# Moving one early load behind a weight piece, and releasing the weight queue on half of a query load

## The chip, the cores and the metric

The kernel runs on one core of a Trainium2 chip. The metric is the device time of one execution in microseconds. The span in a profile, from the first to the last instruction, is some 1.8 us shorter than the time of the same execution.

## The reference, cut to what matters

Gated linear attention over 768 positions, then a mixture of four experts, all of them applied to every row.

```python
f = 1 / (1 + exp(-f_logit))
for t in range(S):                        # B=4, H=8, S=768, D=48
    state = f[:, :, t, :, None] * state + k_t (outer) v_t
    y[:, :, t] = q_t @ state
x = y as [B*S, H*D]                       # 3072 x 384
for e in range(4):
    h = maximum(x @ w1[e], 0)             # 384 -> 1024: "first projection"
    out += p[:, e:e+1] * (h @ w2[e])      # 1024 -> 384: "second projection"
```

The kernel cuts the 768 positions into six chunks of 128 and puts the attention of one chunk beside the expert matmuls of another. Only chunk 0's attention has nothing to hide behind.

## The kernel before: the parts concerned

The engines have these names in the profiles: PE (TensorE, the matmuls), ACT (ScalarE), DVE (VectorE), POOL (GpSimd), SP (SyncE). A small planner orders the instructions of every engine from rough costs. The chunk 0 inputs are loaded by SyncE (SP), one load of 192 KB for each tensor and batch, 192 bytes (one head of one position) in a row. The weights are loaded by GpSimd (POOL), which casts them to bf16 on the way: pieces 0 to 3 are halves of the first two experts' w1, pieces 4 and 5 halves of the first expert's w2 (384 KB each as written), pieces 6 to 10 whole matrices of 768 KB.

```python
def load(c, nm, b, n):                        # c: chunk, nm: f k q v, b: batch
    ins[c, nm, b] = nc.sync.dma_start(out=tl(nm, c, b // 2)[:, hh(b, n), :],
                                      in_=srcs[nm][c, :, b * H:(b + n) * H, :])
    if (c, nm, b) == (1, "f", 1):
        after(ins[c, nm, b], ins["w", w_gate])        # w_gate: piece 8

def load_w(i, e, which, ks, cols):
    ...
    ins["w", i] = nc.gpsimd.dma_start(out=w[:, e, ks, cols], in_=r[e][:, ks, cols])
    if i == 0:
        after(ins["w", 0], ins[0, "q", B - 1])        # weights start here
    if i == w_last:
        after(ins["w", i], ins[1, "k", 0])

def mm_h(c, e, fc, n0, n1):                   # first projection, needs w1
    for kk in range(KD):
        nc.tensor.matmul(out=..., lhsT=w1_sb[:, e, kk, ...], rhs=tl("xT", c)[:, kk, n0:n1], ...)

def mm_o(c, e, nt, fcs, part, cols):          # second projection, needs w2
    for fc in fcs:
        nc.tensor.matmul(out=..., lhsT=tl("h", c, e, ...)[:, fc, ...], rhs=w2_sb[:, e, fc, cols], ...)

for i, x in enumerate("f0 k0 q0 f1 k1 q1 f2 f3 k2 q2 v0 k3 q3 v1 v2 v3".split()):
    add_load(0, x[0], int(x[1]), 1, -1000 + i)
add_load(1, "f", 0, 1, -980, cost=0.1)        # the second chunk's first gate logits
```

`after(x, y)` makes transfer x wait until y has landed.

## Time and profile before

| | before |
|---|---|
| median of 3 runs before the prediction (lowest, highest) | 299.21 us (299.13, 299.32) |
| the execution whose profile was read: time, span | 300.17 us, 298.4 us |
| TensorE (PE) busy in it | 287.4 us |
| PE waiting for weight pieces 0, 1, 4 in it | 0.24, 0.73, 1.15 us |

The prediction quotes the lines of this profile.

### The profile page before, as it was taken

The page shows a single profiled execution, that of the slowest core. Times are in us where ns is not written, and L with a number is a line of the kernel's source. Part 1 is how long each engine was busy: PE and PEld are TensorE (multiplying, and loading weights), DVE is VectorE, ACT ScalarE, POOL GpSimd, SP SyncE. Part 2 cuts the span into 40 slices and gives each one's busy share as a digit, 9 for nine tenths or more (in the row PEclk, how much of TensorE's full clock was granted, in tenths as well). Part 3 has the DMA queues.
Part 4 walks back from the last instruction along what each step waited for, and adds up shares of the span by engine and source line. Part 5 has one row for each costly group of instructions (what it writes and reads, how often), then busy time and mean ns, then how long its engine had stood idle before and what let it go on. Part 6 is the DMA issues. An engine that isn't in the chain of part 4 may idle for free.

```text
span 298.4 us, 5544 instructions
## 1 busy us (share of the span) xinstructions
PE 287.4 (96%) x2132; PEld 170.6 (57%) x2160; DVE 126.8 (43%) x247; ACT 176.1 (59%) x325; POOL 105.5 (35%) x179
## 2 busy tenths in 40 slices
PE   6898899999999999999999999999999999999995
PEld 2466455567777776455555555555555555555553
DVE  6766003585675584036375444332532322201223
ACT  5786573857765676877465574555465544465440
POOL 5397301329498159325548453234220000000000
PEclk9999999999999999999999999999999999999999
DMA  7999999996979979996989962102431100200003
GB/s 146 218 174 195 207 208 188 199 197 168 173 158 193 209 140 181 195 221 118 195 160 205 191 113 35 29 0 64 108 69 38 26 2 26 79 2 0 0 0 108
DMA packets 136462, 36.82 MB, mean 123 GB/s; under 512 B 126812, under 2 KB 135644, under 8 KB 136436
## 3 DMA queue, kind: packets, MB, share of 16 engines
q1 hardware_dynamic: 129348, 30.14, 50.9%
q0 software_dynamic: 7088, 6.33, 13.6%
q8 instruction: 17, 0.28, 0.4%
q14 instruction: 9, 0.07, 0.1%
HBM read 31.51 MB, written 4.72 MB: 121 GB/s over the span
## 4 chain that ended last, share of the span: by engine, by line
PE 88%; DMA 5%; SPq 3%; POOL 1%; issue 1%; DVE 0%
PE ps_m L379 42%; PE ps_m L364 39%; DMA w_sb<-in_moe_w_dram 4%; SPq L232 3%; PE ps_t L320 2%; PE ps_t L335 1%; PE ps_t L331 1%; DMA q<-in_q_dram 1%; PE ps_t L268 1%; POOL w_sb L239 1%; PE ps_t L341 1%; PE ps_t L305 0%; SPq L247 0%; DVE o L386 0%; PE ps_t L360 0%
## 5 line engine op out<-in xcount | busy, mean ns | idle before, releaser
L375 ACT ACTIVATE h<-ps_m 128x512 bf16<-128x512 f32 (+1 forms) x192 | 102.4, 538 | 93.7 <-PE ps_m L364 89.9
L379 PE MATMUL ps_m<-w_sb,h 128*128 128x384 bf16 (+1 forms) x776 | 151.7, 324 | 1.4 <-DMA w_sb<-in_moe_w_dram 1.1
L364 PE MATMUL ps_m<-xT,w_sb 128*128 128x512 bf16 (+1 forms) x670 | 150.1, 341 | 2.1 <-DMA w_sb<-in_moe_w_dram 1.0
L379 PEld LDWEIGHTS <-h 128*128 128x128 bf16 x776 | 75.0, 98 | 60.0 <-DMA w_sb<-in_moe_w_dram 1.6
L386 DVE SCALAR_TENSOR_TENSOR o<-ps_m,pn,o 128x384 f32<-128x384 f32 (+1 forms) x73 | 44.7, 612 | 111.9 <-PE ps_m L379 105.6
L364 PEld LDWEIGHTS <-w_sb 128*128 128x128 bf16 x696 | 65.5, 98 | 43.7 <-DMA w_sb<-in_moe_w_dram 1.4
L296 POOL TENSOR_TENSOR qk<-q,e 128x384 bf16<-128x384 f32 x19 | 22.5, 1189 | 36.3 <-ACT e L288 32.5
L324 DVE TENSOR_TENSOR AT<-ps_t,mask 128x512 bf16<-128x512 f32 x48 | 29.9, 682 | 5.8 <-PE ps_t L320 5.8
L355 POOL TENSOR_TENSOR Sf<-Sf,egs 48x192 f32<-48x192 f32 x40 | 20.1, 503 | 32.6 <-DVE Sf L348 30.6
L288 ACT ACTIVATE e<-ps_t 128x384 f32<-128x384 f32 x48 | 26.6, 665 | 4.1 <-PE ps_t L268 2.9
L373 DVE TENSOR_SCALAR h<-ps_m 128x256 bf16<-128x256 f32 (+1 forms) x40 | 20.0, 510 | 18.3 <-PE ps_m L364 16.1
L296 POOL TENSOR_TENSOR qk<-k,e 128x384 bf16<-128x384 f32 x20 | 20.2, 1015 | 9.3 <-ACT egs L290 4.6
L348 DVE TENSOR_TENSOR Sf<-Sf,ps_t 48x192 f32<-48x192 f32 x40 | 14.0, 351 | 11.4 <-PE ps_t L341 10.7
L239 POOL DMA_DIRECT2D w_sb<-in_moe_w_dram x11 | 9.0, 824 | 21.8 <-DMA k<-in_k_dram 18.5
L356 POOL CAST sb<-Sf 48x192 bf16<-48x192 f32 x40 | 13.6, 340 | 2.6
L388 ACT ACTIVATE o<-ps_m,pn 128x384 f32<-128x384 f32 x22 | 12.8, 581 | 2.8 <-PE ps_m L379 1.7
L293 POOL DMA_DIRECT2D egs<-e x16 | 9.0, 565 | 9.9 <-ACT e L288 9.9
L614 PE MATMUL ps_m<-busy 128*128 128x512 bf16 x32 | 10.5, 427 | 1.6 <-DVE busy L144 1.5
L226 ACT CAST yb<-ps_t 128x384 bf16<-128x384 f32 (+1 forms) x16 | 7.6, 472 | 7.5 <-PE ps_t L335 7.3
L260 ACT ACTIVATE ex<-f 128x768 f32<-128x768 f32 (+1 forms) x14 | 10.5, 748 | 2.3 <-DMA f<-in_f_logit_dram 2.2
L335 PE MATMUL ps_t<-vb,AT 128*128 128x48 bf16 x192 | 11.5, 184 | 0.2 <-DVE vb L228 0.2
L228 POOL CAST vb<-v 128x384 bf16<-128x384 f32 x18 | 9.7, 558 | 3.8 <-DMA v<-in_v_dram 3.7
(54 smaller groups left out, 123.9 us busy)
## 6 DMA issues: line engine op xcount, KB each, us to landing
out_dram<-o SPq DMA_DIRECT2D x23, 192.0 KB, 1.9
w_sb<-in_moe_w_dram POOLq DMA_DIRECT2D x5, 768.0 KB, 19.5
k<-in_k_dram SPq DMA_DIRECT2D x10, 384.0 KB, 4.7
q<-in_q_dram SPq DMA_DIRECT2D x10, 384.0 KB, 5.4
v<-in_v_dram SPq DMA_DIRECT2D x10, 384.0 KB, 5.4
f<-in_f_logit_dram SPq DMA_DIRECT2D x9, 384.0 KB, 5.0
w_sb<-in_moe_w_dram POOLq DMA_DIRECT2D x6, 384.0 KB, 9.4
f<-in_f_logit_dram SPq DMA_DIRECT2D x6, 192.0 KB, 3.8
```

The lines of the kernel that those rows point to most:

```text
L288: nc.scalar.activation(out=o, in_=i, func=AF.Exp, scale=1.0 if j else -1.0)
L296: engines[eng].tensor_tensor(out=tl("qk", c, b)[:, j, :, 0:D].rearrange("t (i r) d -> t i r d", r=2), in0=tl("qk"[j], c, b // 2)[:, hh(b), ...
L324: nc.vector.tensor_tensor(out=tl("AT", c, b)[:, r].rearrange("s i t -> s (i t)"), in0=tl("A", c, b, r).rearrange("s i t -> s (i t)"), in1= ...
L335: nc.tensor.matmul(out=y[:, h * D:(h + 1) * D], lhsT=AT[:, r, i, :], rhs=vb[:, h, :], start=(c == 0), stop=True, skip_group_check=True)
L348: nc.vector.tensor_tensor(out=Sf[rows, b], in0=Sf[rows, b], in1=KV[rows, :, r, :], op=ALU.add)
L355: nc.gpsimd.tensor_tensor(out=Sf[rows, b], in0=Sf[rows, b], in1=eg, op=ALU.mult)
L356: nc.gpsimd.tensor_copy(out=nb[rows, b, :, r * D:(r + 1) * D], in_=Sf[rows, b])
L364: nc.tensor.matmul(out=tl("hp", c, e, fc, n0)[:, n0:n1], lhsT=w1_sb[:, e, kk, fc * 128:(fc + 1) * 128], rhs=tl("xT", c)[:, kk, n0:n1], sta ...
L373: nc.vector.tensor_relu(out=dst, in_=src)
L375: nc.scalar.activation(out=dst, in_=src, func=AF.Relu)
L379: nc.tensor.matmul(out=tl("op", c, e, nt, part)[:, cols], lhsT=tl("h", c, e, half_of(c, nt * T))[:, fc, nt * T:(nt + 1) * T], rhs=w2_sb[:, ...
L386: nc.vector.scalar_tensor_tensor(out=o, in0=op, scalar=pe, in1=o, op0=ALU.mult, op1=ALU.add)
```

## The change

Its intent is to bring the first weights to PE sooner, in two ways. The last query load of chunk 0 is cut into two halves of four heads, and the weight queue waits for the first of them alone. The second chunk's first gate logits, 192 KB not needed before 50 us, no longer run beside the first weights: they wait until piece 6 has landed.

```diff
     def load(c, nm, b, n):
-        ins[c, nm, b] = nc.sync.dma_start(out=tl(nm, c, b // 2)[:, hh(b, n), :],
-                                          in_=srcs[nm][c, :, b * H:(b + n) * H, :])
+
+        for h in ((H // 2, H // 2) if (c, nm, b) == (0, "q", B - 1) else (n * H,)):
+            h0 = 0 if (c, nm, b) not in ins else h
+            op = nc.sync.dma_start(out=tl(nm, c, b // 2)[:, hh(b).start + h0:hh(b).start + h0 + h, :],
+                                   in_=srcs[nm][c, :, b * H + h0:b * H + h0 + h, :])
+            ins.setdefault((c, nm, b), op)
+        if (c, nm, b) == (1, "f", 0):
+            after(ins[c, nm, b], ins["w", 6])
@@
-    add_load(1, "f", 0, 1, -980, cost=0.1)
@@
     for i, (e, which, ks, cols) in enumerate(pieces):
+        if i == 7:
+            add_load(1, "f", 0, 1, -454.5, deps=wd[2, 1], cost=0.1)
```

## The prediction

> **What bounds the kernel now.** I read the page first: engine shares, slices, the chain that ended last. TensorE (PE) is busy for 287.4 of 298.4 us at a granted clock of 9 tenths or more in every slice, and the chain is PE for 88%.
>
> ```profile
> PE 287.4 (96%) x2132; PEld 170.6 (57%) x2160; DVE 126.8 (43%) x247; ACT 176.1 (59%) x325; POOL 105.5 (35%) x179
> PE   6898899999999999999999999999999999999995
> PE 88%; DMA 5%; SPq 3%; POOL 1%; issue 1%; DVE 0%
> ```
>
> The reader is to see that only the first slices of the PE row fall short of 9. So nothing but a wait of PE in the first 35 us can be won. I therefore took the chain in order of time, its first 75 us:
>
> ```profile
> 11.59 3.59 DMA q<-in_q_dram
> 15.18 0.30 issue
> 15.47 3.24 POOL w_sb L239 x4
> 18.72 12.54 DMA w_sb<-in_moe_w_dram
> 31.26 0.05 issue
> 31.30 1.47 PE ps_m L379 x8
> ```
>
> This is the path that sets the end: the last query load of chunk 0 (issued at 11.59, landed at 15.18) releases the weight queue on POOL; the fifth piece (number 4, the first half of the first expert's w2) is issued as the fifth there and lands at 31.26; PE then starts the second matmuls (L379) and is never again short of work. The timeline of PE shows how long it stood still before:
>
> ```profile
> 21.05 1.16 PE L364 MATMUL ps_m<-xT,w_sb 128*128 128x256 bf16 x9 [0.24 <-DMA w_sb<-in_moe_w_dram]
> ...
> 23.43 0.50 PE L364 MATMUL ps_m<-xT,w_sb 128*128 128x256 bf16 x3 [0.73 <-DMA w_sb<-in_moe_w_dram]
> ...
> 31.30 1.47 PE L379 MATMUL ps_m<-w_sb,h 128*128 128x384 bf16 x8 [1.15 <-DMA w_sb<-in_moe_w_dram]
> ```
>
> The bracket is PE's idle time: 0.24 + 0.73 + 1.15 = 2.12 us, all for pieces 0, 1 and 4. That sum is the ceiling of what earlier weights can bring. The waits of PE after 31.3 us come to one entry, this same 1.1 us; from 60 us on the view of waits lists none.
>
> The view of DMA issues, in windows around one issue each, gives landings as start plus time to landing: piece 0 at 15.47 + 5.5 = 21.0, piece 1 at 23.3, piece 2 at 25.6, piece 3 at 28.1, piece 4 at 31.3, piece 5 at 32.9, piece 6 at 36.7, piece 7 at 40.6, piece 8 at 44.2, piece 9 at 48.1, piece 10 at 59.4. The window about the first weight issue also holds the load that the change moves:
>
> ```profile
> w_sb<-in_moe_w_dram POOLq DMA_DIRECT2D x1, 384.0 KB, 5.5
> f<-in_f_logit_dram SPq DMA_DIRECT2D x1, 192.0 KB, 13.3
> ```
>
> The second chunk's first gate logits are issued at 15.08 and land at 28.4: all their 192 KB run beside pieces 0 to 3, before piece 4 lands.
>
> **What the Trainium skill says.** "DMA: Bandwidth & Descriptors", section "Issuing engines are not separate DMA queues": transfers from different engines end on the same 16 DMA engines and interleave. The trace agrees: between 20.5 and 31 us the DMA share is 1.18 to 1.39 and the rate 185 to 228 GB/s, while two queues run. Same page, section "Anatomy of one DMA": most of a fixed cost of about 2 us is the receipt at the end. The trace has stores landing in a median 1.9 us, and loads in 3.2 to 3.8 us under load; so a half load can't land much sooner by being half, only by standing earlier in the queue. "Perfetto Trace Analysis", section "DMA Optimizations": splitting may let some work start sooner if the DMA engines are generally idle. Here they are not (225, 233 and 187 GB/s in the half microseconds from 14 us), so I expect little of the split itself.
>
> **The change part by part.**
> (a) The split. The key load before it lands at 11.15 + 3.2 = 14.35 and the query load at 15.18, so 192 KB take 0.83 us of the queue. The half that ends first should land about 0.83 / 2 = 0.4 us sooner, at 14.8. POOL has been free since 12.24 + 1.00 = 13.24, so weight issues start near 15.05 in place of 15.47. Cost: one more SP issue (such issues take 0.4 to 1.3 us), with the value loads behind it; their landings (4.2 to 5.3 us after issue) are queued data, not issue time. The second half feeds a product on DVE that starts at 15.71, half a microsecond after the landing; no cost. In the built program the weights do wait on the first half, and each later load on the semaphore of one load later than before, all of them landed by then.
> (b) The gate logits leave. 192 KB (196.6 thousand bytes) at the 190 GB/s of 21 to 27 us is 196.6 / 190 = 1.03 us of DMA time that pieces 0 to 4 no longer share. Most of its benefit is there at piece 4; by piece 1 perhaps 0.4 us, as about half of it has then been sent.
> (c) They come back behind piece 6 (about 35.5 us), before the second gate load, which still waits for piece 8. Nothing else stands on the SP queue from 15 to 44.6 us, so blocking it costs nothing. Pieces 7 to 10 get the 1.0 us back and end about 0.4 us earlier than before.
> (d) The order of instructions. PE's is the same up to the middle of the second chunk, where two small matmuls (L268) go ahead of three transposes; ACT and DVE swap some evictions from there on. The amount of PE work is unchanged. I give this 0.
>
> Sum: piece 4 lands 0.4 + 1.0 = 1.4 us sooner, at 29.9. Would PE be ready? Its work ahead ended at 25.76 + 4.40 = 30.16, of which 0.73 us was the wait for piece 1. Piece 1 comes 0.4 + 0.4 = 0.8 us sooner, the piece 0 wait gives at most 0.24, so PE is ready at some 29.3 to 29.5, still before 29.9. So PE gains the full 1.4 us.
>
> Does it keep it? PE needs piece 5 at 33.9 (the half projections behind the first two, landed 32.9), piece 6 at 39.75 (36.7), piece 7 at 42.99 (40.6), piece 8 at 50.1 (44.2), piece 9 at 52.1 (48.1), piece 10 at 62.45 (59.4). Taking 1.4 us from the first column, and 1.4 (pieces 5, 6) or 0.4 us from the landings, leaves at least 1.0 us everywhere: the tightest are piece 5 with 1.0 and piece 7 with 41.6 against 40.2, 1.4 us. The second gate load landed at 49.4 and ACT reads it at 52.77; minus 1.4 it is still 2 us behind. So 299.21 - 1.4 = 297.8 us, 0.5% less.
>
> **The rivals.**
> First, the logits were hidden anyway: if they took slots that the weight queue could not use, removing them frees nothing. For it: the rate falls to 69 and 58 GB/s from 17.0 to 18.0 us with both queues loaded, so the engines are not always full. Against it: from 20.5 us on the share is over 1.2 without a gap, and pieces 1 to 3 are 2.3 to 2.5 us apart where 393 KB at 190 GB/s would take 2.07. It would leave (a) alone, 298.8 us.
> Second, PE takes over: chunk 0's own attention sets when the first projections can run. The transposed copies of batches 1 and 2 are done at 20.9 and of batch 3 at 22.8, and the value product at 20.44 stands ahead in PE's order. If pre-projection work can't move by more than the 0.3 us there, PE is ready at about 29.9: the gain is 1.2 to 1.3 us rather than 1.4, 298.0 us. If instead piece 4 is sooner than I think, this limit and the 2.12 us ceiling stop the gain: 297.1 us.
> Third, something in the middle gives it back: piece 7 late behind the returned logits, or a PE wait from the new order of evictions. For it: PE waits for nothing from 60 us on, so any change of order can only hurt there. Against it: margins of 1 us and more, and only 12 of the 4315 rows in PE's order differ. It would make 298.3 to 299.2 us.
>
> **Range and chances.** 1.4 us with (a) between 0.1 and 0.6 and (b) between 0.6 and 1.3 gives 0.7 to 1.9; adding a loss of up to 0.4 us at the lower end gives 297.0 to 298.9 us for 8 in 10. A gain over 2% (6.0 us) is three times the idle time there is: 0.01. A loss over 2% would need a new stall of 6 us, with loads issued in nearly the same order: 0.01. Within 2%: 0.98.
>
> **What would show it.** In the profile after: the first weight issue on POOL near 15.0 us; piece 4's landing, that is PE's first L379 matmul, at 29.9 in place of 31.3, with a wait of 0.3 to 0.7 us ahead of it; the moved load issued near 35.5 us; no PE wait over 0.2 us from there to the end; the end 1.4 us sooner. Step (a) is wrong if POOL starts within 0.1 us of 15.47; (b) is wrong if the distance from POOL's start to L379 (31.30 - 15.47 = 15.8 us) doesn't shrink to about 14.8; the keeping is wrong if L379 starts sooner by more than the end does.

## The result, and the profile after

| | before | after |
|---|---|---|
| median of 6 runs each, same chip | 299.17 us (298.57 to 300.38) | 298.67 us (298.32 to 298.92) |
| span of the profiled execution | 298.4 us | 296.9 us |

The ratio is 0.998, with a 95% interval of 0.996 to 0.9999. A ratio here is the mean time of one kernel's runs over that of the other's of the same rounds, so not quite the ratio of the medians. Executions over 1.5% slower than the fastest of the same kernel are left out of the means. The gain is real but small: 0.5 us of the forecast 1.4.

The two profiles say something else. Their spans differ by 1.5 us, as forecast. That is three times what the medians differ by.

The page of the changed kernel: the busy time of each engine, and the shares of the engines in the chain (the work that ended last, followed back from the last instruction to what released each step):

```profile
PE 287.3 (97%) x2132; PEld 170.7 (58%) x2160; DVE 127.6 (43%) x249; ACT 175.7 (59%) x323; POOL 105.6 (36%) x179
PE 91%; DMA 4%; SPq 3%; issue 1%; POOL 0%; DVE 0%
```

PE's work is the same; less of the chain is DMA (4% in place of 5%). The changed kernel's chain in order of time (start, us, what) where the weights enter it:

```profile
14.63 0.30 issue
14.93 0.92 POOL w_sb L245
15.85 7.52 DMA w_sb<-in_moe_w_dram
23.36 0.05 issue
23.41 0.50 PE ps_m L370 x3
```

The chain before went through four weight issues to piece 4 and to the second projections at 31.30. This one goes through a single issue and then the second: the transfer that is issued at 15.85 and lands at 23.36 is piece 1, the second half of the first expert's w1. From there on this stretch of the chain is PE alone. The timeline of PE in the changed kernel (start, us, engine and line, matmuls, idle time before them and what ended it; L370 is the first projection, L385 the second, which were L364 and L379 before; the edits of the experiments shift these numbers by a few lines):

```profile
21.54 1.16 PE L370 MATMUL ps_m<-xT,w_sb 128*128 128x256 bf16 x9 [1.15 <-DMA w_sb<-in_moe_w_dram]
23.41 0.50 PE L370 MATMUL ps_m<-xT,w_sb 128*128 128x256 bf16 x3 [0.22 <-DMA w_sb<-in_moe_w_dram]
29.97 1.46 PE L385 MATMUL ps_m<-w_sb,h 128*128 128x384 bf16 x8
```

There is no bracket on the third line: piece 4 landed at 29.2, and PE no longer waits for it. Piece 0 landed at 21.5 and piece 1 at 23.4, where they had landed at 21.0 and 23.4 before, although POOL had begun 0.54 us sooner.

### The profile page after: what moved, and what is told of

It reads as the page before. It is cut to its first block, busy times and chain, and to the rows that moved or that the text cites. A ratio compares the mean times of both kernels' runs of the same rounds, so it can differ in the third digit from the quotient of the medians.

```text
span 296.9 us, 5547 instructions
## 1 busy us (share of the span) xinstructions
PE 287.3 (97%) x2132; PEld 170.7 (58%) x2160; DVE 127.6 (43%) x249; ACT 175.7 (59%) x323; POOL 105.6 (36%) x179
## 3 DMA queue, kind: packets, MB, share of 16 engines
q0 software_dynamic: 7088, 6.33, 13.8%
## 4 chain that ended last, share of the span: by engine, by line
PE 91%; DMA 4%; SPq 3%; issue 1%; POOL 0%; DVE 0%
PE ps_m L385 42%; PE ps_m L370 41%; SPq L235 3%; DMA w_sb<-in_moe_w_dram 3%; PE ps_t L326 2%; PE ps_t L341 1%; PE ps_t L337 1%; PE ps_t L347 1%; PE ps_t L274 1%; DMA q<-in_q_dram 1%; POOL w_sb L245 0%; PE ps_t L311 0%; SPq L253 0%; DVE o L392 0%; PE ps_t L366 0%
## 5 line engine op out<-in xcount | busy, mean ns | idle before, releaser
L370 PE MATMUL ps_m<-xT,w_sb 128*128 128x512 bf16 (+1 forms) x670 | 150.1, 341 | 2.5 <-DMA w_sb<-in_moe_w_dram 1.4
L385 PE MATMUL ps_m<-w_sb,h 128*128 128x384 bf16 (+1 forms) x776 | 151.5, 324 | 0.2
L385 PEld LDWEIGHTS <-h 128*128 128x128 bf16 x776 | 75.1, 98 | 58.6
L370 PEld LDWEIGHTS <-w_sb 128*128 128x128 bf16 x696 | 65.5, 98 | 44.1 <-DMA w_sb<-in_moe_w_dram 1.8
L302 POOL TENSOR_TENSOR qk<-q,e 128x384 bf16<-128x384 f32 x19 | 22.5, 1187 | 36.6 <-ACT e L294 30.1
L330 DVE TENSOR_TENSOR AT<-ps_t,mask 128x512 bf16<-128x512 f32 x48 | 29.9, 682 | 6.1 <-PE ps_t L326 6.1
L379 DVE TENSOR_SCALAR h<-ps_m 128x256 bf16<-128x256 f32 (+1 forms) x40 | 20.0, 510 | 19.3 <-PE ps_m L370 17.0
```

The costliest lines, as they stand in the source:

```text
L302: engines[eng].tensor_tensor(out=tl("qk", c, b)[:, j, :, 0:D].rearrange("t (i r) d -> t i r d", r=2), in0=tl("qk"[j], c, b // 2)[:, hh(b), ...
L330: nc.vector.tensor_tensor(out=tl("AT", c, b)[:, r].rearrange("s i t -> s (i t)"), in0=tl("A", c, b, r).rearrange("s i t -> s (i t)"), in1= ...
L370: nc.tensor.matmul(out=tl("hp", c, e, fc, n0)[:, n0:n1], lhsT=w1_sb[:, e, kk, fc * 128:(fc + 1) * 128], rhs=tl("xT", c)[:, kk, n0:n1], sta ...
L379: nc.vector.tensor_relu(out=dst, in_=src)
L385: nc.tensor.matmul(out=tl("op", c, e, nt, part)[:, cols], lhsT=tl("h", c, e, half_of(c, nt * T))[:, fc, nt * T:(nt + 1) * T], rhs=w2_sb[:, ...
```

## The experiments

Theory A: the profile of before that the prediction was read from was a slow execution. In a usual one PE doesn't wait for piece 4; the end is set by the landing of piece 1, and the change is worth what it does to piece 1. Rival B: the profile was a usual one, the change wins 1.4 us at the second projections, and some of it is lost later.

The first four ran on one chip together, with 11 runs of before (median 299.18 us); the next four with 11 of before (median 299.91, lowest 299.22, highest 301.06, so a noisier job); the last four with 12 of before (median 299.09).

### The kernel before again (no edit)

> The kernel before, unchanged, as a null. Theory A (the profile that the prediction was read from was a slow execution of before, 300.17 us against a median of 299.2; in a usual one TensorE waits less for weight pieces): the profile here shows a span near 297.5 us where the earlier one had 298.4, and a wait before the first second-projection matmul of under 0.5 us in place of 1.15. Rival B (the usual execution has the same 2.1 us of waits and the changed kernel loses its gain later): span near 298.4 again when the time is near 299.2, wait again 1.1 us. Ratio to before 1.000 within 0.2%.

Measured: median 299.34 us, ratio 1.0004 (0.9992 to 1.0016), profiled span 297.4 us. PE's timeline of this execution of the kernel before:

```profile
21.30 1.16 PE L364 MATMUL ps_m<-xT,w_sb 128*128 128x256 bf16 x9 [0.97 <-DMA w_sb<-in_moe_w_dram]
23.84 0.50 PE L364 MATMUL ps_m<-xT,w_sb 128*128 128x256 bf16 x3 [0.89 <-DMA w_sb<-in_moe_w_dram]
30.40 1.46 PE L379 MATMUL ps_m<-w_sb,h 128*128 128x384 bf16 x8
```

The wait for piece 4 is gone. The second projections start 0.90 us sooner than in the first profile, and the span is 1.0 us shorter. Theory A holds: the 11 timed runs of before beside it have spans of 297.0 to 297.9 us, none near 298.4. Slow ones are not rare, though: of the 29 timed runs of before in the first measurement and in the first and last jobs, two took more than 300 us, and of the 11 in the noisier job five did.

### The changed kernel again (no edit)

> The changed kernel, unchanged. Both theories: 0.997 to 0.999 of before. Theory A: TensorE does not wait for piece 4 at all, it waits for pieces 0 and 1 (together 0.5 to 1.5 us) and the first second-projection matmul starts 6.6 us after piece 1 has landed. Rival B: starts sooner than that and the gain is lost after 40 us.

Measured: 298.40 us, ratio 0.998 (0.9968 to 0.9992), span 296.7. In its trace the projections that need piece 1 start at 23.18 and the second ones at 29.74, again 6.56 us later, with no wait between:

```profile
23.18 0.50 PE L370 MATMUL ps_m<-xT,w_sb 128*128 128x256 bf16 x3 [0.23 <-DMA w_sb<-in_moe_w_dram]
29.74 1.46 PE L385 MATMUL ps_m<-w_sb,h 128*128 128x384 bf16 x8
```

Against the usual execution of before, the start moved by 30.40 - 29.74 = 0.66 us (0.43 us with the first trace of after). That is the size of the medians' difference (0.5 and 0.8 us), though single traces of one kernel differ by as much.

### Only the split

```diff
-        if (c, nm, b) == (1, "f", 0):
-            after(ins[c, nm, b], ins["w", 6])
@@
+    add_load(1, "f", 0, 1, -980, cost=0.1)
@@
-        if i == 7:
-            add_load(1, "f", 0, 1, -454.5, deps=wd[2, 1], cost=0.1)
```

(against the changed kernel; PE's order is that of before)

> The query load split, the gate logits left where they were. Theory A: the weight issues start some 0.4 us sooner but pieces 0 and 1 land within 0.3 us of before because the value loads hold the queue until about 17.5 us; time 0.999 to 1.001 of before. Rival (the split brings its 0.4 us): 0.9985 of before.

Measured: 299.47 us, ratio 1.0004 (0.9992 to 1.0017). The two timelines of this kernel, POOL and PE:

```profile
14.64 2.47 POOL L243 DMA_DIRECT2D w_sb<-in_moe_w_dram  x3 [0.42 <-DMA q<-in_q_dram]
```

```profile
24.06 0.50 PE L368 MATMUL ps_m<-xT,w_sb 128*128 128x256 bf16 x3 [1.00 <-DVE pn L261]
```

POOL starts 0.87 us sooner than in the usual trace of before (15.51), and still piece 0 lands at 21.4 and piece 1 at 24.0 (21.3 and 23.8 there). The profile puts PE's wait down to a DVE instruction that ended at 24.02, when piece 1 landed as well (24.0). That instruction doesn't hold these matmuls: in both traces of before they start while it still runs (at 23.43 and 23.84, where it ends at 23.65 and 23.91). The split alone wins nothing.

### Only the move

```diff
-        for h in ((H // 2, H // 2) if (c, nm, b) == (0, "q", B - 1) else (n * H,)):
+        for h in (n * H,):
```

> The gate logits moved behind piece 6, the query load whole. Theory A: piece 4 lands 1.0 to 1.5 us sooner than in the kernel before, TensorE does not wait for it, the whole gain of the change is here: 0.997 to 0.999 of before. Rival (it takes both): 0.999 to 1.000, half of the change's gain.

Measured: 298.75 us, ratio 0.9994 (0.9973 to 1.0015), one of six runs at 300.58 us with a clock of 0.994. The ratio is outside what theory A had said. Because of that run I repeated it, beside the changed kernel, in the last job:

> Only the move, repeated, since its first interval (0.9973 to 1.0015, one run of six at a clock of 0.994) left open whether the split adds anything. Theory A (the split adds nothing, weight packets need some 2 us from their issue and ramp slowly): within 0.1% of the changed kernel. Rival (the split gives a part): 0.1 to 0.2% slower than the changed kernel.

> The changed kernel once more, as the yardstick for the next three on one chip. 0.997 to 0.999 of before; the first second-projection matmul 6.6 us after the start of the projections that need piece 1, the rest of the program 267.0 us from there.

Measured: the move alone 298.17 us, ratio 0.9973 (0.9957 to 0.999); the changed kernel 298.44 us, ratio 0.9981 (0.9964 to 0.9999). PE's timeline of the move alone in that job:

```profile
20.57 1.16 PE L370 MATMUL ps_m<-xT,w_sb 128*128 128x256 bf16 x9 [0.34 <-DMA w_sb<-in_moe_w_dram]
22.45 0.50 PE L370 MATMUL ps_m<-xT,w_sb 128*128 128x256 bf16 x3 [0.22 <-DMA w_sb<-in_moe_w_dram]
29.01 1.46 PE L385 MATMUL ps_m<-w_sb,h 128*128 128x384 bf16 x8
```

In the last job the move by itself does all that the change does, and the first job doesn't contradict it. Whether it is a little faster than the change (0.8 thousandths in one job, slower by 1.4 thousandths in the other) the runs don't settle.

### Twice the load beside the weights

The kernel before, with the gate logits of two batches in the one early load:

```diff
     def load(c, nm, b, n):
+        if (c, nm, b) == (1, "f", 1):
+            return
+        if (c, nm, b) == (1, "f", 0):
+            n = 2
@@
-        if (c, nm, b) == (1, "f", 1):
+        if (c, nm, b) == (1, "k", 0):
             after(ins[c, nm, b], ins["w", w_gate])
```

> The kernel before with the suspected cost doubled: the gate logits of two batches (384 KB) beside the first weights, every engine's order unchanged but the one load of the second batch. Theory A (the end is the landing of piece 1 or, where piece 4 comes over 6.5 us after it, of piece 4, plus a constant of 267 us from the first second-projection matmul): the extra 192 KB delay whichever of them binds by 0.5 to 1.0 us; that matmul starts at 30.9 to 31.6 us and the time is 1.002 to 1.0035 of before. Rival (the logits are hidden, and the change gains from the shifted order of instructions after 60 us): 1.000.

Measured: 300.92 us against 299.91, ratio 1.0023 (0.9997 to 1.0049). The interval just reaches 1, but the trace shows the mechanism. PE's timeline:

```profile
21.96 1.16 PE L368 MATMUL ps_m<-xT,w_sb 128*128 128x256 bf16 x9 [0.97 <-DMA w_sb<-in_moe_w_dram]
25.01 0.50 PE L368 MATMUL ps_m<-xT,w_sb 128*128 128x256 bf16 x3 [1.39 <-DMA w_sb<-in_moe_w_dram]
31.91 1.47 PE L383 MATMUL ps_m<-w_sb,h 128*128 128x384 bf16 x8 [0.17 <-DMA w_sb<-in_moe_w_dram]
```

Piece 1 lands 3.1 us after piece 0 (25.0 and 21.9). With one such load it was 2.4 to 2.7 us (23.4 and 21.0; 23.8 and 21.3; 24.0 and 21.4), with none 1.9 us in all five traces. So each 192 KB in that place costs piece 1 about 0.6 us, not 1.03. The second projections start later than was expected (31.91 us; 30.9 to 31.6), but not all of that is the load's doing: POOL starts 0.47 us later than in the usual trace of before (15.98 against 15.51), and the last query load was issued late (12.07 against 11.31) before there was any extra load.

### A much earlier release

```diff
         if i == 0:
-            after(ins["w", 0], ins[0, "q", B - 1])
+            after(ins["w", 0], ins[0, "q", 2])
```

(against the changed kernel; every engine keeps its order)

> The changed kernel with the weights released by the third query load in place of the half of the fourth; same order on every engine. POOL is free from some 13.1 us, so the weight issues start 1.7 us sooner. Theory A (weight packets do not flow while the queue of small-packet loads is full, so the start of the issue does not matter): the first weight packets still show at 16.5 to 17 us, piece 0 lands at 20.9 to 21.6 us, time 0.997 to 0.999 of before, as the changed kernel. Rival (each issue has a fixed start-up of some 1.8 us): first packets near 15 us, piece 0 lands near 20 us, the value loads later, time 0.995 to 0.997 or, if attention is late, no gain.

Measured: 308.11 us, ratio 1.0246 (1.0214 to 1.0277). Neither was right: I had expected nothing or a gain, and it costs 2.5%. The rival had the value loads later, but not that they cost anything like this. The chain of this kernel in order of time, and one line of ACT's timeline:

```profile
14.30 12.72 DMA v<-in_v_dram
27.02 0.02 issue
...
27.46 0.48 ACT yb L226
27.94 0.05 issue
27.99 0.50 PE ps_t L366 x3
```

```profile
27.04 0.51 ACT L226 CAST vb<-v 128x384 bf16<-128x384 f32 x1 [8.69 <-DMA v<-in_v_dram]
```

Here the last value load of chunk 0, issued by 14.3, lands at 27.0; in the first profile of before, ACT reads it at 19.1. PE stands still for 6.69 us behind this, and its mean granted clock between 20 and 30 us is 0.53, a part of the loss whose size no run separates. The whole loss lies before the second projections: they start at 37.99, and the rest of the span takes 304.9 - 37.99 = 266.9 us, as in the changed kernel. The queues in a half microsecond in the middle of that (22.5 to 23.0 us; packets, MB, and the time that the packets took as a share of that of the 16 DMA engines, which goes over 100% where packets overlap; q0 carries the weights, q1 SP's loads), first this kernel, then the changed kernel at 20.5 to 21.0 us:

```profile
q0 software_dynamic: 79, 0.08, 93.7%
q1 hardware_dynamic: 79, 0.02, 27.5%
```

```profile
q0 software_dynamic: 104, 0.10, 124.5%
```

Packet for packet the queues take turns, but a weight packet has 1 KB and a load packet 192 bytes: the load gets 192 of 1,216 bytes, about a sixth. The wait on the last query load is thus what keeps the attention's own loads fast in this kernel. Releasing the weights 0.5 to 0.9 us sooner than in the kernel before was harmless, 2.0 us sooner was not. The experiment also says when weights begin to flow. The issue starts at 13.45 and the first weight packets show in the half microsecond from 15.5, some 2 us later. In the other traces it is much the same: issues at 14.64, 14.93 and 15.23 have first packets in the half microsecond from 16.5, and 15.51 in that from 17.0. After that it takes until 18 to 20.5 us to come near the full rate of some 104 packets in half a microsecond. Of the half microsecond and more that the split wins in issue, little is left in packets: by 20.0 us the weight queue had moved 364 packets with only the split against 339 and 327 in the kernel before, and 393, 422 and 420 with both against 432 and 460 with only the move. Why the sooner issue brings no more packets, no run separates.

### Finer pieces

The changed kernel with the first expert's w1 in four pieces in place of two (pieces behind it renumbered):

```diff
-    pieces = [(e, 1, every, slice(i * F // 2, (i + 1) * F // 2)) for e in range(2) for i in range(2)]
+    pieces = [(0, 1, every, slice(i * F // 4, (i + 1) * F // 4)) for i in range(4)]
+    pieces += [(1, 1, every, slice(i * F // 2, (i + 1) * F // 2)) for i in range(2)]
```

> The changed kernel with the first expert's first weights in four pieces in place of two. Theory A (the grain of pieces 0 and 1 binds TensorE): the first projection starts near 20.9 us in place of 21.3 to 21.5 and the first second-projection matmul 0.3 to 0.8 us sooner than in the changed kernel, then limited by w2's first half, which lands near 29; time 0.995 to 0.9975 of before. Rival (chunk 0's attention or w2's first half binds already): same as the changed kernel, 0.998.

Measured, in the noisy job: 299.58 us against 299.91, ratio 0.9978 (0.9949 to 1.0008), with runs from 298.43 to 303.51. In the trace of its fastest run the second projections start at 29.47, sooner than in the changed kernel, and the span is 296.7 us all the same. I repeated it in the last job, and once more with the query load whole:

> Four pieces for the first expert's first weights, repeated beside the changed kernel. Its first trace has no weight wait on TensorE after 19.6 us, but the attention of chunk 0 ran 0.9 us later there than in other traces. Theory A (weights bound the changed kernel, attention is next): 0.1 to 0.3% faster than the changed kernel. Rival (attention is as late as the weights, so nothing is won): equal to it.

> Four pieces and the move, the query load whole. Theory A: as quarters within 0.1%, since with four pieces the first one lands near 20 us and TensorE is not ready for it before 20.5. Rival: 0.15% slower.

Measured: 299.10 us, ratio 0.9998 (0.9983 to 1.0013), and 299.82 us, ratio 1.0018 (1.0002 to 1.0034). It gives away what the move won, and theory A's gain isn't there. The second of the two is 0.2% slower than the first, as the rival had it; the intervals overlap, so whether the split helps with finer pieces stays open. PE's timeline of the first of these two, then its weight queue from 20.5 to 21.0 us, then that of the changed kernel in the same job:

```profile
23.79 0.50 PE L370 MATMUL ps_m<-xT,w_sb 128*128 128x256 bf16 x3 [1.33 <-DMA w_sb<-in_moe_w_dram]
30.34 1.46 PE L385 MATMUL ps_m<-w_sb,h 128*128 128x384 bf16 x8
```

```profile
q0 software_dynamic: 152, 0.08, 132.6%
```

```profile
q0 software_dynamic: 103, 0.10, 124.2%
```

The first quarter lands at 19.6, but rows half as long move 0.08 MB where the longer ones move 0.10 (0.38 against 0.51 MB from 19.5 to 22 us), and the fourth quarter lands at 23.7 where piece 1 landed at 23.1. The rule stays the same: 23.79 + 6.55 = 30.34. But that isn't the whole loss. The planner orders some instructions otherwise here, and PE waits again at about 61 us (0.7 us for ACT, 0.3 us for a weight piece) where the changed kernel waits for nothing. From the second projections to the end these traces take 267.2 us (the first run), 267.6 and 267.2.

The last kernel had both the finer pieces and the early release:

> Both: four pieces and the early release. Theory A: as quarters, 0.995 to 0.9975. Rival (start-up latency): 0.993 to 0.995, with w2's first half landing 1 us sooner.

Measured: 305.33 us, ratio 1.0165 (1.013 to 1.0199): the starved value loads again (the last one is read at 25.04 by ACT, which had waited 5.85 us for it).

### What the traces agree on

| trace | POOL starts weights | piece 0, piece 1, piece 4 landed | projections needing piece 1 | second projections | span | span less the column before |
|---|---|---|---|---|---|---|
| before, first profile | 15.47 | 21.0, 23.4, 31.3 | 23.43 | 31.30 | 298.4 | 267.1 |
| before, again | 15.51 | 21.3, 23.8, 29.6 | 23.84 | 30.40 | 297.4 | 267.0 |
| only the split | 14.64 | 21.4, 24.0, 29.8 | 24.06 | 30.62 | 297.6 | 267.0 |
| only the move | 15.23 | 21.1, 22.9, 28.8 | 22.98 | 29.54 | 296.6 | 267.1 |
| only the move, again | 15.21 | 20.5, 22.4, 28.2 | 22.45 | 29.01 | 296.0 | 267.0 |
| after | 14.93 | 21.5, 23.4, 29.2 | 23.41 | 29.97 | 296.9 | 266.9 |
| after, again | 14.81 | 21.2, 23.1, 28.9 | 23.18 | 29.74 | 296.7 | 267.0 |
| after, third | 14.79 | 21.2, 23.1, 28.9 | 23.17 | 29.74 | 296.7 | 267.0 |
| two gate loads | 15.98 | 21.9, 25.0, 31.9 | 25.01 | 31.91 | 299.0 | 267.1 |

The last column is constant to 0.2 us in these nine traces (the finer pieces, with another order, have up to 267.6): nothing that happens after the second projections begin matters to this change. Their start is the start of the piece 1 projections plus 6.56 us of PE work, unless piece 4 is later than that, as in the first and the last row. Rival B falls.

## Why the prediction was wrong, point by point

**The starting point.** "PE then starts the second matmuls (L379) and is never again short of work", with 1.15 us of waiting for piece 4 ahead of it, was true of the profiled execution only: this is the step that failed. It took 300.17 us when the runs took 299.13 to 299.32; that should have been a warning, and I passed over it. In the second trace of before PE waits about 1.9 us for pieces 0 and 1 (0.97 and 0.89) and not at all for piece 4; the trace with only the split, which keeps the gate load in its place, shows no wait for piece 4 either. The forecast subtracted a gain read at piece 4 of a slow execution from the median of usual ones. The profile after does agree with the forecast against that one profile (span 1.5 us less); it agrees because 1.0 us of it is the difference between two executions of the same kernel. Nor does it count for the forecast that the second projections start at 29.97, where 29.9 was named: that was to be the landing of piece 4 with a wait of 0.3 to 0.7 us, and there is no wait. The agreement is luck.

What was different in that execution shows in its queues; that this is what made it slow is likely, but rests on this one trace (22.5 to 23.0 us, q0 the weights, q1 the gate logits):

```profile
q0 software_dynamic: 86, 0.08, 92.3%
q1 hardware_dynamic: 88, 0.02, 29.2%
```

And the usual execution of before, where most of the same load passes from 20.0 to 21.5 us in one burst (here 20.5 to 21.0):

```profile
q1 hardware_dynamic: 440, 0.08, 85.7%
q0 software_dynamic: 37, 0.03, 38.1%
```

In the slow one the 1,024 small packets took turns with weight packets over some 7 us and slowed the weights from about 104 to 80 packets in each half microsecond. In the usual one most of them took three half microseconds, and the weights lost about (105 - 53) + (105 - 37) + (105 - 72) = 153 packets there; at 105 in half a microsecond that is 0.7 us, near the 0.6 us of the doubling experiment. With only the split, most of the load also passes in a burst (722 packets from 19.5 to 21.0 us). What decides between burst and turns I can't tell from the runs.

**Step (a), the split.** Its first half was right: POOL was expected near 15.05 and starts at 14.79 to 14.93. Its second half, that pieces 0 and 1 land 0.4 us sooner for it, failed: measured 0, in the split alone and in the comparison of the change with the move alone. The working took an earlier issue for an equally earlier landing. From the start of POOL to piece 0 it is 5.3 to 5.9 us with the whole load (five traces) and 6.4 to 6.7 us with the split one (four traces, pieces of the same size): all that the issue wins is lost again before the landing. A start-up of some 2 us and a slow ramp lie between an issue and its data, and the value loads are still in the queue then; that this is the reason is likely, not shown. The section "Anatomy of one DMA" of the Trainium skill, on which the prediction drew for a half load, speaks of transfers issued from GpSimd; no run here separates such a cost for SP's loads.

**Step (b), the move.** The mechanism was right, the size was not. 1.03 us at piece 4 took the whole of the bytes as lost to the weights; 0.6 us is what piece 1 loses, and piece 1 is what counts. The prediction's sign for this step, the distance from POOL's start to the second projections, shrinks as named against the slow profile (15.8 to 15.0), but not against the usual execution of before (14.9): the split moves one end of it. With the query load whole it does shrink, from 14.9 to 14.3 and 13.8.

**The readiness of PE** was the step that turned the two into a gain: "Piece 1 comes 0.4 + 0.4 = 0.8 us sooner". Measured against a usual execution: 0.4 to 0.7 us (23.8 to 23.4, 23.1 and 23.1), all of it from the move. The second rival named the limit ("PE takes over") but put it down to the attention; it was the landing of piece 1.

**Steps (c), (d) and the keeping** held. No wait of PE is listed from 31 us to the end in the profile after; SP issues the moved load at 34.8 us; the constant 267 us says that the new order of evictions costs nothing.

Sum with measured terms: 0 for the split, 0.4 to 0.7 us for the move, nothing lost later. The medians of the three jobs with the changed kernel differ by 0.5, 0.8 and 0.65 us, those with the move alone by 0.4 and 0.9.

**The range** has a slip: a gain of 1.9 us at most gives 299.21 - 1.9 = 297.3 us, not 297.0. And where the prediction says that two queues run between 20.5 and 31 us, the second does so only until the gate logits land at 28.4; the rates quoted for the stretch before that stand (185 to 203 GB/s up to 28 us).

## What to carry to other kernels

Before reading a gain off a profile, compare the time of the profiled execution with the median: a wait of 1 us seen in an execution that is itself 1 us slow is not there to be won. Profile the same kernel twice when the change is worth less than 1%. Where weights and activations share the DMA engines, as here, a wait that holds the weights back can be a guard for the activations: moving a load that nobody needed yet out of the weights' way won 0.4 to 0.9 us, starting the weights 2 us sooner lost 2.5%.

## What the Trainium skill lacked or had wrong

- "DMA: Bandwidth & Descriptors", section "Queues, rings and completion order", says that each DMA engine takes turns between its queues packet by packet, where such a packet holds several descriptors. The packets of the profile here are single rows of 192 B or 1 KB. One trace has equal turns (79 weight packets and 79 load packets in half a microsecond with the early release), another doesn't (37 and 440 in the usual execution of before); whether the second contradicts the page is not shown, as no view tells which rows make one packet of the page. The page doesn't say when it is one or the other, nor what equal turns mean for a queue of small rows: about a sixth of the bytes, and a last value load that lands at 27 us where it is read at 19 us in the first profile of before.
- The same page, section "Latency and other measured facts", has about 1 us to the first byte for transfers issued from GpSimd, and doesn't say from when it counts. Here the first weight packets appear in the half microsecond that begins 1.3 to 2.1 us after the issue has started, which is 0.4 to 1.1 us after it has ended (an issue takes 0.92 us). The page has nothing on what follows: the full rate comes only 1.5 to 3.5 us after the first packets, with another queue busy at first.
- The same page, "Specifications", gives 512 B as the least for the full rate. Weight rows of 512 B as written (1 KB as read, with a cast) moved 0.38 MB from 19.5 to 22 us where rows of 1 KB moved 0.51; from 18 to 19.5 us, as they started, it was 0.26 against 0.25 MB.
- No page says how far one execution of a kernel may stand from the next: two profiles of the unchanged kernel differ by 1.0 us in span (298.4 and 297.4) through the landing of one weight piece.
